# A new hand-written order for a fused cross-attention and PReLU kernel on one Trainium2 core

## The chip, the cores and the metric

The kernel runs on one core of one Trainium2 chip. A core has a matrix engine (TensorE, in the profile PE, with its weight loads as PEld), a vector engine (DVE), a scalar engine (ACT), a general engine (POOL) and a queue engine (SP). Each works through its own list of instructions in order and waits on semaphores of the others. PE reads SBUF and writes PSUM, which has eight banks of 128 x 512 float32; DVE and ACT read PSUM, POOL does not touch it here. The metric is the device time of one execution in microseconds (us), the median of several runs; lower is better.

## The reference

```
scores  = scale * x @ state^T          # per batch b and head h: 512 x 32
xread   = softmax(scores) @ state      # 512 x 64
scores2 = scale * state @ x^T          # 32 x 512
sread   = softmax(scores2) @ x         # 32 x 64
y   = concat([xread, sread], tokens), heads side by side   # (8 * 544) x 512
h   = y @ w_in                         # 512 -> 2048
g   = max(h, 0) + alpha * min(h, 0)
out = g @ w_out                        # 2048 -> 512
```

There are 8 batches, 8 heads, 512 tokens of width 64 and 32 states a head. `x`, `state`, `w_in`, `w_out`, `alpha` and `out` are float32; the kernel works in float16 with float32 sums.

## The kernel before

**Attention.** The 512 tokens of a batch and its states meet once, in a product of scores `sc` (L326), laid out as 128 rows (4 heads x 32 states) by 1024 columns. From it come both softmaxes. Over the states: DVE transposes blocks (`sb`, L357), takes maxima (`smax`), POOL subtracts (`ssh`), ACT takes the exponential (`sexp`), DVE sums (`ssum`), POOL scales (`snorm`, L387), DVE transposes back (`wb`, L397) into the tile `aT`. Over the tokens: DVE takes maxima (`tx`), ACT scales them (`ty`) and takes the exponential with its sum (`te`), DVE inverts the sum (`tsum`), POOL or ACT scales (`tn`), a DMA on SP's queue transposes (`tt`, tile `e2T`), and PE makes the state reads (`rd`, L461, tile `sr_ps`).

**First layer.** `xread @ w_in` is never made as such. PE first makes the products of states and `w_in`, `m` (L486: 8 heads, four column blocks of 512; `m.b.f` is batch b, block f, 8 matmuls), which ACT or DVE casts to SBUF (`mo`, L508). Then each of 16 tiles of h is two matmuls over `aT` (`F.b.jc`, L519). ACT makes the negative part (`N`, L551) and DVE the PReLU (`G`, L569). The state reads of all batches go through the first layer together, as a ninth batch (`F.8`, L528).

**Second layer.** Batch 0 is a plain product (`S`, L588). Batches 1 to 8 use seven products `P` (L668) in place of eight: POOL makes four sums of g for each (`A`, L645, three by itself, one as an accumulating DMA, L621) and sums of `w_out` (`T`); ACT and DVE put the results together (`Q`), and SP stores them (`W`). Pieces of batch 7 are made apart (`M`, L717, and `MO`), so that they can be done late.

**Order.** A string of some 1,180 steps sets everything. A step such as `m.6.1.4.1` names the work and, where it is a PSUM tile, its banks (4 and 1); a last letter names the engine (`a` ACT, `v` DVE, `p` POOL, `d` a DMA). `m` without banks and `sc` use one tile of two banks, tagged `two`. The steps are recorded in the order of the string, and each engine gets its own in that order. So the string also sets what stands behind what on each queue: the loads of x (`lx`) and of the weights (`wi`, `wo`) and the accumulating DMAs are issued from POOL, the transposing DMAs (`xd`, `tt`) and nearly all stores from SP. `Z` steps are matmuls on zeros that only keep PE busy.

`m` and `sc` use PE in tiles of 64 x 32, `rd` and the transposes of the states in tiles of 128 x 64, all the rest in its whole 128 x 128.

Of the kernel before, what the change touches and what calls it, by code (L numbers as in the profile page):

```python
# [17 lines left out]
lx0 id lst stc xc.1.v xc.0.a oma wi.0 lx.1 Z.1.20 stt.0 Z.2.9 xt.0.1.0.1 xt.0.0.0.2 xo.0.1.0.v  # L18
xo.0.0.0.v sto.a Z.0.7 sc.0.0 Z.0.6 xt.0.1.1.3 xt.0.0.1.4 str.0.5 sb.0.0 xo.0.0.1.v xo.0.1.1.a Z.1.4
sc.0.1 smax.0.0 str.1.0 sro.0.a wi.1 sb.0.1 wo.0 smax.0.1 wi.2 ssh.p.0.0 sro.1.a sexp.0.0 Z.1.3 sc.0  # L20
m.0.0.1.2 ssh.p.0.1 mo.0.0.a.0 Z.5.5 m.1.0.3.4 m.2.0.5.0 tm.0 mo.2.0.a.0 ssum.0.0 sexp.0.1
mo.1.0.a.0 mo.2.0.a.1 wo.1 Z.1.12 m.3.0.1.5 Z.3.7 xt.1.1.0.3 snorm.p.0.0 mo.1.0.v.1 te.0.1
mo.3.0.a.1 ssum.0.1 wb.0.0 xt.1.0.0.4 xo.1.1.0.v te.0.0 xo.1.0.0.v wi.3 xt.1.1.1.0 snorm.p.0.1 Z.3.9
f.0.0.0.5 mo.0.0.a.1 xo.1.1.1.v xt.1.0.1.3 wo.2 f.0.2.0.4 tsum.0 m.1.1 wb.0.1 mo.3.0.a.0 xo.1.0.1.v
m.0.1.0.2 mo.1.1.v.0 tn.0.0 mo.0.1.v.0 f.0.2.1 f.0.0.1 mo.1.1.a.1 mo.0.1.a.1 f.0.1.0.1 f.0.1.1
F.0.3.3 m.4.0 N.0.0 N.0.1 F.0.5.2 N.0.2 F.0.4.0 G.0.0 G.0.1 N.0.3 G.0.2 F.0.7.5 N.0.5 N.0.4 G.0.3
S.0.1.0.1 mo.4.0.a.0 S.0.0.0.4 mo.4.0.a.1 G.0.4 S.0.0.1 S.0.1.1 lx.2 N.0.7 m.0.2.3.0 sc.1 G.0.5
mo.0.2.a.0 S.0.2.0.2 wo.3 G.0.7 m.1.2.5.3 mo.0.2.a.1 mo.1.2.a.0 S.0.2.1 sb.1 F.0.6.0 xd.2 mo.1.2.a.1
F.0.8.5 N.0.6 F.0.9.3 tm.1 S.0.1.2 N.0.8 S.0.2.2 S.0.0.2 G.0.6 S.0.1.3 te.1.1 te.1.0 N.0.9 F.0.11.0
# [89 lines left out]
def kernel(  # L119
# [17 lines left out]
    nc = tc.nc  # L137
# [695 lines left out]
```

## Time and profile before

| | |
|---|---|
| median of 3 runs | 210.05 us (210.01 to 210.38) |
| the profiled execution: first to last instruction | 208.5 us |
| median less that span | 1.55 us |
| PE busy | 200.2 us |
| DVE, ACT, POOL busy | 175.2, 145.5, 180.9 us |
| granted PE clock | 1.000 |

The profiled execution has a span and no time of its own beside it. What lies around the span is taken as 1.55 us, by the median. The busy times overlap; a busy PE counts the pipelined end of each matmul too, so the spacing of two groups is what one of them costs.

### The profile page before, as it was taken

Reading aid. Unit: us, or ns where it says so; the run is one execution under the profiler, and the core shown is the slowest. Engines: PE = TensorE matmul, PEld = TensorE weight load, DVE = VectorE, ACT = ScalarE, POOL = GpSimd, SP = SyncE. Lnnn points to the kernel's source line nnn. Section 1 sums busy time; section 2 is a strip of 40 time slices with the busy share of each in tenths; the row PEclk is TensorE's granted clock in tenths of the full one; section 3 lists DMA queues with packets and bytes.
Section 4 is the critical chain, followed back from the end, with each engine's and each line's share of the span. In section 5 each row is a group of like instructions: output and inputs, shape, how many; then the busy total and the mean of one; then the engine's idle time right before and its main releaser. Section 6 shows DMA issues by size and latency. Waiting matters only on the chain.

```text
span 208.5 us, 5136 instructions
## 1 busy us (share of the span) xinstructions
PE 200.2 (96%) x2034; PEld 135.3 (65%) x2034; DVE 175.2 (84%) x273; ACT 145.5 (70%) x291; POOL 180.9 (87%) x119
## 2 busy tenths in 40 slices
PE   7789999999999999999999999999999999999993
PEld 6554344346557775766677776666678777888882
DVE  1697998999999999999999999998995987744431
ACT  4298996699998899988889579778654545451110
POOL 7579948999999999999999999979996972969960
PEclk9999999999999999999999999999999999999999
DMA  6999999599979949999997166035401144234143
GB/s 148 177 204 208 205 203 149 103 132 191 218 144 142 116 58 212 206 126 165 183 225 100 43 146 166 24 82 151 104 0 53 23 78 154 37 63 156 50 153 104
DMA packets 44793, 27.11 MB, mean 130 GB/s; under 512 B 22097, under 2 KB 42465, under 8 KB 44769
## 3 DMA queue, kind: packets, MB, share of 16 engines
q0 software_dynamic: 14192, 12.03, 38.5%
q1 hardware_dynamic: 29872, 14.23, 31.1%
q10 hardware_dynamic: 704, 0.52, 0.8%
q8 instruction: 16, 0.26, 0.5%
q14 instruction: 9, 0.07, 0.1%
HBM read 17.31 MB, written 8.91 MB: 126 GB/s over the span
## 4 chain that ended last, share of the span: by engine, by line
PE 70%; DVE 14%; ACT 5%; DMA 4%; POOL 3%; issue 2%; DVEq 0%; POOLq 0%
PE p L668 41%; PE h L519 18%; DVE gp L569 8%; DMA w_in_sb<-in_moe_w_in_dram 4%; PE h L528 3%; PE m_ps L486 3%; PE sr_ps L461 2%; ACT m L508 1%; DVE aT L397 1%; ACT neg L551 1%; DVE m L508 1%; POOL s L645 1%; ACT e L424 1%; POOL an L387 1%; PE o L588 1%
## 5 line engine op out<-in xcount | busy, mean ns | idle before, releaser
L551 ACT ACTIVATE neg<-h 128x512 f32<-128x512 f32 (+1 forms) x144 | 78.5, 583 | 27.4 <-PE h L519 18.5
L569 DVE SCALAR_TENSOR_TENSOR gp<-neg,oma_sb,h 128x512 f16<-128x512 f32 x128 | 89.0, 735 | 6.7 <-ACT neg L551 6.4
L519 PE MATMUL h<-aT,m 128*128 128x512 f16 x250 | 68.6, 379 | 0.3 <-DVE gp L569 0.3
L645 POOL TENSOR_TENSOR s<-gp,s 128x1024 f16<-128x1024 f16 x28 | 65.7, 2393 | 1.2 <-DVE gp L569 0.6
L668 PEld LDWEIGHTS <-gp 128*128 128x128 f16 x432 | 41.7, 98 | 13.9 <-issue 1.9
L668 PEld LDWEIGHTS <-s 128*128 128x128 f16 x368 | 35.2, 98 | 12.7 <-POOL s L645 1.7
L668 PE MATMUL p<-ws,s 128*128 128x256 f16 x248 | 37.3, 273 | 0.2 <-POOL s L645 0.2
L645 POOL TENSOR_TENSOR s<-gp 128x1024 f16<-128x1024 f16 x14 | 31.6, 2260 | 6.5 <-DVE gp L569 6.4
L519 PEld LDWEIGHTS <-m 128*128 128x128 f16 x250 | 23.6, 98 | 16.1 <-issue 3.3
L668 PE MATMUL p<-ws,gp 128*128 128x256 f16 x224 | 33.6, 273 | 0.0
L508 ACT CAST m<-m_ps 128x512 f16<-128x512 f32 x51 | 28.8, 600 | 4.8 <-PE m_ps L486 3.6
L668 PE MATMUL p<-w_out_sb,gp 128*128 128x256 f16 x208 | 30.6, 273 | 0.0
L371 POOL TENSOR_TENSOR ts<-ts,mx 128x1024 f32<-128x1024 f32 (+1 forms) x9 | 17.1, 1905 | 6.0 <-DVE mx L365 6.0
L668 PE MATMUL p<-w_out_sb,s 128*128 128x256 f16 x120 | 18.3, 273 | 0.0
L387 POOL TENSOR_TENSOR an<-ts,r 128x1024 f16<-128x1024 f32 (+1 forms) x9 | 16.3, 1808 | 1.8 <-DVE r L382 1.8
L588 PE MATMUL o<-w_out_sb,gp 128*128 128x512 f16 x64 | 16.6, 380 | 0.1
L621 POOL DMA_DIRECT2D gp<-gp x14 | 13.2, 962 | 3.4 <-issue 2.9
L569 DVE SCALAR_TENSOR_TENSOR gs<-neg,oma_sb,h 128x256 f16<-128x256 f32 x16 | 7.2, 478 | 8.2 <-ACT neg L551 8.2
L486 PE MATMUL m_ps<-w_in_sb,stT 64*32 64x512 f16 x256 | 11.7, 383 | 0.3 <-DMA w_in_sb<-in_moe_w_in_dram 0.2
L588 PEld LDWEIGHTS <-gp 128*128 128x128 f16 x64 | 5.9, 98 | 8.1 <-issue 1.3
L424 ACT ACTIVATE e<-sc,nb 128x512 f16<-128x512 f32 x16 | 11.0, 693 | 0.1
L699 ACT COPY p<-p 128x512 f32<-128x512 f32 x11 | 6.5, 588 | 6.4 <-PE p L668 6.4
(76 smaller groups left out, 248.9 us busy)
## 6 DMA issues: line engine op xcount, KB each, us to landing
out_dram<-c SPq DMA_DIRECT2D x27, 256.0 KB, 3.1
xg<-in_x_dram POOLq DMA_DIRECT2D x7, 512.0 KB, 8.7
gp<-gp POOLq DMA_DIRECT2D x14, 256.0 KB, 3.6
w_in_sb<-in_moe_w_in_dram POOLq DMA_DIRECT2D x4, 512.0 KB, 11.8
w_out_sb<-in_moe_w_out_dram POOLq DMA_DIRECT2D x4, 512.0 KB, 13.1
out_dram<-osb SPq DMA_DIRECT2D x4, 256.0 KB, 3.0
out_dram<-c SPq DMA_DIRECT2D x3, 128.0 KB, 2.1
x<-in_x_dram SPq DMA_DIRECT2D x1, 256.0 KB, 3.2
```

Source lines behind the costliest of these rows:

```text
L371: engine(e).tensor_tensor(ts, ts, over_blocks(cols(live["mx", b], j, S // N)), ALU.subtract)
L387: engine(e).tensor_tensor(blocks(cols(live["an", b], j, S)), blocks(cols(live["ts", b], j, S)), over_blocks(cols(live["r1", b], j, S // N) ...
L424: nc.scalar.activation(live["e2", b][:, g, :, :], live["sc", b][:, :, :, g, :].rearrange("p r j s -> p (r j) s"), EXP, bias=live["nb", b][ ...
L486: nc.tensor.matmul(t[N * k : N * (k + 1), :], st_head(b, h)[64 * r : 64 * r + 64, :], w_in_sb[64 * r : 64 * r + 64, c, 512 * f : 512 * (f ...
L508: copier(e)(m_tile(b)[:, f, g, :], live["mp", b, f][g])
L519: nc.tensor.matmul(h.rearrange("p (r j s) -> p r j s", r=2, j=2), ms[b][:, f, g, 128 * j : 128 * (j + 1)], weights(b, g), start=(g == 0), ...
L551: nc.scalar.activation(neg, h, RELU, bias=0.0, scale=-1.0)
L569: nc.vector.scalar_tensor_tensor(gt, negs.pop((b, jc)), oma_sb[:, jc : jc + 1], h, ALU.mult, ALU.add)
L588: nc.tensor.matmul(outs[b, q], token_cols(b, jc, q), w_out_sb[:, jc, :], start=(jc == 0), stop=(jc == n_jc - 1),)
L621: nc.gpsimd.dma_start(gp[:, 1, 0], gp[:, 1, 1], accum_op=ALU.add)
L645: engine(e).tensor_tensor(t, x, y, op)
L668: nc.tensor.matmul(chains[chain][:, t, :], lhs, rhs[:, i, :], start=(opens and i == 0 and t == 0), stop=(i == half_k - 1), skip_group_chec ...
```

## The change

The string of steps is replaced. The work is the same, but for two matmuls on zeros fewer (82 to 80). Three scalings of token weights go from POOL to ACT (`tn`), two scalings of token maxima from DVE to ACT (`tm` becomes `tx` and `ty`), and of the copies out of PSUM three results, three state reads and one transpose go from DVE to ACT; the cast of the first states goes to ACT as well. Nine casts of `m` change from DVE to ACT and nine the other way.

```diff
-P.3.3.2 N.4.9 A.4.3.1.p P.4.1.1 G.4.10 P.3.3.3 P.3.4.0 G.4.9 P.4.1.2 G.4.12 P.3.4.1 A.4.1.0.d
-Q.3.c12.v m.6.3 m.6.0.4.5 A.4.2.0.p mo.6.3.a.0 rd.4.3 mo.6.0.v.0 W.Q.3.c12 mo.6.3.a.1 rd.5.0 tsum.6
-wb.5 W.Q.3.c22 tn.6.1.a sc.7 P.3.4.2 mo.6.0.a.1 P.4.1.3 rdo.5.v ssh.p.6 tx.7 P.3.4.3 Q.4.p1.a
...
+Q.3.c12.v W.Q.3.c12 tsum.6 W.Q.3.c21 m.6.1.4.1 mo.6.1.a.0 mo.6.1.v.1 rd.4.2 A.4.3.0.p m.6.3.0.5 mo.6.3.a.1
+mo.6.3.v.0 rd.5.3 rdo.5.a m.6.2.4.1 mo.6.2.a.0 mo.6.2.a.1 sc.7 m.6.0.0.5 mo.6.0.a.0 mo.6.0.a.1 P.4.1.0.3
...
-M.7.2.0.3 M.7.1.0.4 P.8.5.1 W.Q.8.c11 P.8.7.0 P.8.5.2 P.8.7.1 P.8.5.3 P.8.7.2 Q.8.p5.v M.7.1.1
-M.7.2.1 P.8.7.3 M.7.1.2 P.8.3.0 Q.8.c22.v M.7.2.2 M.7.1.3 P.8.3.1 WA.Q.8.c22 MO.7.1.v P.8.4.0
-P.8.3.2 W.MO.7.1 P.8.4.1 P.8.3.3 P.8.4.2 Q.8.c12.v M.7.2.3 P.8.4.3 MO.7.2.v W.Q.8.c12 Q.8.c21.a
-WA.MO.7.2 W.Q.8.c21
+P.8.3.1 P.8.3.2 P.8.3.3 Q.8.c12.v W.Q.8.c12 P.8.4.1 P.8.4.2 P.8.4.3 Q.8.c21.a W.Q.8.c21 M.7.2.0.3 M.7.2.1
+M.7.2.2 M.7.2.3 MO.7.2.v WA.MO.7.2
...
-    def first_states_cast():
+    def first_states_cast(e):
         live["st0"] = consts.tile([128, 2, D], F16, name="st0")
-        nc.vector.tensor_copy(live["st0"], st0_32)
+        copier(e)(live["st0"], st0_32)
```

PE goes from whole tiles into the small tiles of `m`, `sc`, `rd` and the state transposes, and back, 33 times before and 25 times now. With the changes between 64 x 32 and 128 x 64 counted too, its tiling changes 72 times before and 64 times now.

On ACT, around the state products of batch 6 (`m_6` is the cast product, `m_ps6_f_g` block f and half g of it in PSUM, `XS` the state reads, `neg_5_jc` the negative part of tile jc of batch 5), before:

```order
L508 CAST m_6_1840<-m_ps6_3_2079 128x512 x2
L440 ACTIVATE e2_6_2002<-e2_6_2002,r2_6_2003 128x512
L508 CAST m_6_1840<-m_ps6_0_1_2089 128x512
L699 COPY p1_4_2209<-p1_4_2034 128x512
L472 CAST XS_86<-sr_ps4_2101 128x4x32
L551 ACTIVATE neg_5_0_2228<-h_5_0_2217 128x512
```

and now:

```order
L499 CAST m_6_2087<-m_ps6_1_0_2077 128x512
L499 CAST m_6_2087<-m_ps6_3_1_2126 128x512
L463 CAST XS_86<-sr_ps5_2137 128x4x32
L499 CAST m_6_2087<-m_ps6_2_0_2171 128x512
L499 CAST m_6_2087<-m_ps6_2_1_2172 128x512
L499 CAST m_6_2087<-m_ps6_0_0_2200 128x512
L499 CAST m_6_2087<-m_ps6_0_1_2201 128x512
L463 CAST XS_86<-sr_ps4_2090 128x4x32
L542 ACTIVATE neg_5_5_2252<-h_5_5_2225 128x512
```

All four blocks of batch 6 are now cast in one run, with both state reads among them, ahead of the first negative part of batch 5; before, blocks 2 and 1 stood elsewhere.

On SP's queue, from the first result of batch 1 on (`xT_4` is the transposed x of batch 4, `e2T_2` the transposed token weights of batch 2), before:

```order
L579 DMA out_0_dram<-c11_1_1068 256x1x256
L304 DMA_TRANSPOSE xT_4_1071<-xg_4_901 128x16x128
L446 DMA_TRANSPOSE e2T_2_1145<-e2_2_778 128x8x128
L446 DMA_TRANSPOSE e2T_3_1324<-e2_3_1161 128x8x128
L579 DMA out_0_dram<-c22_1_1217 256x1x256
```

and now:

```order
L570 DMA out_0_dram<-c11_1_1094 256x1x256
L437 DMA_TRANSPOSE e2T_2_1249<-e2_2_763 128x8x128
L295 DMA_TRANSPOSE xT_4_1297<-xg_4_901 128x16x128
L295 DMA_TRANSPOSE xT_5_1317<-xg_5_987 128x16x128
L437 DMA_TRANSPOSE e2T_3_1333<-e2_3_1203 128x8x128
```

`xT_4` has moved behind `e2T_2`, which waits for ACT's scaling of the token weights of batch 2; `xT_5` has moved up to it.

More of the change, by code (lines that the diff above doesn't have):

```diff
@@ new lines @@
+mo.4.0.a.1 S.0.1.0.2 S.0.1.1 m.0.2.3.1 mo.0.2.a.0 mo.0.2.a.1 S.0.0.1 sc.1 tx.1 T.0.1.p m.1.2.3.5 sb.1
+mo.1.2.a.0 mo.1.2.a.1 F.0.7.0 N.0.7 G.0.7 smax.1 ssh.p.1 ty.1 F.0.8.1 F.0.11.3 N.0.11 G.0.11 te.1.0 te.1.1
+T.1.0.p tsum.1 N.0.8 G.0.8 S.0.1.2 S.0.2.0.5 S.0.2.1 S.0.2.2 F.0.9.0 N.0.9 G.0.9 S.0.0.2 m.0.3 mo.0.3.a.1
+mo.0.3.a.0 S.0.1.3 S.0.0.3 F.0.10.3 m.1.3 mo.1.3.v.1 N.0.10 G.0.10 sexp.1 ssum.1 S.0.2.3 snorm.p.1 F.0.13.0
+tn.1.0.a F.0.14.1 S.0.1.4 S.0.2.4 N.0.14 G.0.14 mo.1.3.a.0 F.0.12.3 N.0.12 G.0.12 N.0.13 G.0.13 S.0.2.5
@@ new lines @@
+T.1.1.p S.0.0.4 S.0.0.5 tn.1.1.a F.0.15.1 N.0.15 m.2.1 mo.2.1.a.1 mo.2.1.a.0 S.0.3.0.3 S.0.2.6 S.0.0.6 G.0.15
+S.0.2.7 O.0.2.a W.O.0.2 tt.1 T.3.0.p T.2.0.p m.3.3.1.0 mo.3.3.a.0 mo.3.3.a.1 sc.2 S.0.0.7 O.0.0.a W.O.0.0 wb.1
+F.1.2.5 tx.2 ty.2 sb.2 lx.3 N.1.2 G.1.2 F.1.1.1 N.1.1 F.1.3.0 te.2.1 N.1.3 S.0.1.5 S.0.1.6 S.0.1.7 O.0.1.a
+smax.2 G.1.1 ssh.p.2 F.1.9.4 G.1.3 te.2.0 N.1.9 G.1.9 S.0.3.1 S.0.3.2 F.1.8.5 F.1.0.2 N.1.0 G.1.0 F.1.10.1
+N.1.10 S.0.3.3 G.1.10 N.1.8 G.1.8 sexp.2 ssum.2 rd.0.0 rdo.0.a m.2.3 rd.1.4 F.1.6.2 rdo.1.a F.1.7.1 N.1.7
@@ new lines @@
+P.1.6.0 F.2.15.0 G.2.10 P.1.6.1 N.2.15 G.2.15 F.2.13.4 N.2.13 G.2.13 mo.3.2.a.0 P.1.2.2 F.2.0.3 P.1.2.3
+Q.1.c11.v xd.3 W.O.0.1 sc.3 m.4.1.0.2 sb.3 tx.3 tn.2.1.a N.2.0 G.2.0 mo.4.1.a.0 mo.4.1.a.1 A.1.2.1.p P.1.6.2
+P.1.6.3 Q.1.u.a tn.2.0.a A.1.1.0.d F.2.9.5 A.1.1.1.d P.1.5.0.0 A.1.4.0.p P.1.5.1 F.2.12.2 P.1.5.2 F.2.2.4
+W.Q.1.c11 P.1.5.3 smax.3 ty.3 N.2.9 P.1.7.0 P.1.7.1 G.2.9 N.2.2 N.2.12 G.2.12 G.2.2 Q.1.p5.a te.3.0 T.2.1.p
+P.1.7.2 te.3.1 tsum.3 P.1.7.3 Q.1.c22.v F.2.11.5 F.2.5.2 N.2.11 G.2.11 N.2.5 G.2.5 A.1.4.1.p P.1.3.0 P.1.3.1
@@ new lines @@
+P.1.3.2 ssh.p.3 sexp.3 ssum.3 tt.2 rd.2.4 rdo.2.a m.4.3.5.3 mo.4.3.a.0 mo.4.3.a.1 xd.4 sc.4 tn.3.0.a xd.5
+P.1.4.0 P.2.2.0.4 P.1.4.1 tn.3.1.a tt.3 F.2.6.3 N.2.6 sb.4 tx.4 F.2.14.5 N.2.14 G.2.14 A.2.3.0.p ty.4 G.2.6
+te.4.1 te.4.0 P.1.3.3 T.3.1.p P.1.4.2 P.1.4.3 Q.1.c21.a P.2.1.0.2 P.2.2.1 P.2.2.2 snorm.p.3 wb.3 m.3.1.3.5
+m.5.1 P.2.1.1 mo.3.1.a.1 mo.3.1.a.0 P.2.2.3 smax.4 Q.1.c12.v F.3.1.5 N.3.1 G.3.1 F.3.10.3 N.3.10 G.3.10
+F.3.8.1 N.3.8 G.3.8 P.2.1.2 P.2.1.3 Q.2.p1.a Q.2.c11.v F.3.11.5 N.3.11 G.3.11 W.Q.1.c21 W.Q.1.c12 W.Q.1.c22
@@ new lines @@
+mo.4.2.a.0 mo.4.2.a.1 snorm.p.4 wb.4 F.3.15.0 F.4.2.5 N.4.2 G.3.14 sb.5 tx.5 A.2.4.0.p P.2.3.0 N.3.15 G.3.15
+P.2.4.3 A.3.3.1.p Q.2.c21.a F.4.7.1 N.4.7 G.4.7 ty.5 te.5.1 te.5.0 G.4.2 P.2.3.1 P.2.3.2 F.4.12.2 P.2.3.3
+Q.2.c12.v F.4.1.0 N.4.1 G.4.1 tsum.5 F.4.14.1 N.4.14 G.4.14 F.4.4.5 N.4.4 G.4.4 F.4.0.3 N.4.0 G.4.0 tn.5.1.a
+F.4.3.4 N.4.3 G.4.3 P.3.1.0.0 P.3.1.1 N.4.12 G.4.12 F.4.11.1 N.4.11 G.4.11 P.3.1.2 P.3.2.0.5 P.3.1.3 Q.3.p1.a
+smax.5 P.3.2.1 F.4.13.4 N.4.13 P.3.2.2 m.5.3.2.3 mo.5.3.a.0 m.5.0 mo.5.0.a.0 tsum.4 mo.5.3.v.1 P.3.2.3
@@ new lines @@
+Q.3.c11.v W.Q.3.c11 W.Q.2.c21 F.4.6.1 N.4.6 G.4.6 G.4.13 mo.5.0.a.1 F.4.5.2 N.4.5 G.4.5 F.4.10.3 N.4.10 G.4.10
+W.Q.2.c12 A.3.3.0.p A.3.2.0.p tn.5.0.a tt.5 P.3.6.0 P.3.6.1 lx.7 A.3.2.1.p P.3.6.2 P.3.6.3 Q.3.u.a sc.6 xd.7
+m.7.3.4.1 mo.7.3.v.1 tx.6 sb.6 tn.4.0.a m.5.2.2.5 mo.5.2.a.1 tn.4.1.a tt.4 mo.5.2.a.0 P.3.7.0 P.3.7.1 F.4.9.1
+N.4.9 P.3.7.2 G.4.9 A.3.1.0.d P.3.5.0.5 A.3.1.1.d A.3.4.0.p smax.6 ssh.p.5 sexp.5 P.3.5.1 P.3.7.3 P.3.5.2
+P.3.5.3 Q.3.p5.a Q.3.c22.v F.4.15.1 N.4.15 ty.6 F.4.8.2 N.4.8 A.4.3.1.p P.3.3.0 P.3.3.1 mo.7.3.a.0 G.4.15
@@ new lines @@
+Q.4.c11.v W.Q.4.c11 A.4.1.0.d ssh.p.6 sexp.6 ssum.6 N.5.15 te.7.0 F.5.7.2 F.5.3.0 N.5.3 P.4.6.0 G.5.15 P.4.6.1
+F.5.6.4 N.5.6 G.5.6 A.4.2.1.p P.4.6.2 F.5.1.1 tn.6.1.p snorm.p.6 N.5.7 G.5.7 te.7.1 tsum.7 P.4.6.3 P.4.5.0.5
+P.4.5.1 P.4.5.2 P.4.5.3 Q.4.u.a P.4.7.0 P.4.7.1 G.5.3 N.5.1 G.5.1 tn.6.0.a wb.6 F.5.8.1 N.5.8 G.5.8 F.5.4.0
+Q.4.p5.a P.4.7.2 P.4.7.3 Q.4.c22.v N.5.4 G.5.4 smax.7 F.5.9.2 N.5.9 G.5.9 tn.7.0.a F.5.13.1 N.5.13 G.5.13
+F.5.10.4 N.5.10 G.5.10 P.4.4.0 P.4.4.1 A.4.4.0.p P.4.3.0 P.4.3.1 P.4.4.2 A.4.4.1.p tn.7.1.a F.6.2.2 tt.7 N.6.2
```

139 lines of the change are left out of this document (49 added, 90 removed).

## The prediction, made before the changed kernel was run

> **What bounds the kernel now.** I read the busy times first, then what PE waited for after its start, and then PE's own timeline beside the chain of waits.
>
> ```profile
> span 208.5 us, 5136 instructions
> PE 200.2 (96%) x2034; PEld 135.3 (65%) x2034; DVE 175.2 (84%) x273; ACT 145.5 (70%) x291; POOL 180.9 (87%) x119
> PE p L668 <- POOL s L645: 0.2, 1, 0.2
> ```
>
> The last row is the whole answer for PE's waits between 25 and 205 us: one wait of 0.2 us. From 25 us on PE sets the time, although DVE and POOL are nearly full too. The same matmuls are made after the change, so it can win only what PE spends beside them: the start, changes of tiling, and the end after the last matmul. Each new wait of PE costs its full length.
>
> ```profile
> 66.22 0.60 PE L668 MATMUL p<-ws,s 128*128 128x256 f16 x4
> 66.75 0.41 PE L486 MATMUL m_ps<-w_in_sb,stT 64*32 64x512 f16 x8
> 67.09 0.61 PE L668 MATMUL p<-ws,s 128*128 128x256 f16 x4
> ...
> 75.92 0.68 PE L461 MATMUL sr_ps<-e2T,xg 128*64 128x32 f16 x32
> 76.53 0.63 PE L486 MATMUL m_ps<-w_in_sb,stT 64*32 64x512 f16 x16
> 77.09 0.61 PE L668 MATMUL p<-w_out_sb,gp 128*128 128x256 f16 x4
> ...
> 89.56 0.41 PE L326 MATMUL sc<-xT,stT 64*32 64x256 f16 x16
> 89.78 0.40 PE L486 MATMUL m_ps<-w_in_sb,stT 64*32 64x512 f16 x8
> 71.63 3.06 PE p L668 x28
> 80.75 2.16 PE h L519 x10
> ```
>
> The last two rows, from the chain of waits, give 3.06/28 = 0.109 us for a P matmul and 2.16/10 = 0.216 for one of h. Four P from 66.22 end their issue at 66.66; `m` starts 0.09 later. Its 8 matmuls take 0.34 to the next group. Sixteen take 0.56 (76.53 to 77.09), so 8 more cost 0.22 and leaving costs 0.34 - 0.22 = 0.12. One visit to small tiles costs 0.21, one change of tiling about 0.105. From `sc` into `m`, which have the same tiling, nothing is lost (89.56 to 89.78 is 0.22).
>
> **The change part by part.** *Joined stretches.* After the first tile of h of batch 1, the old string changes PE's tiling 43 times and the new one 32 times: 11 x 0.105 = **-1.15 us**. The visits fall more, but `m` and `rd` now alternate inside them, and each alternation is paid as well. Bounds: 0, if a joined stretch waits inside for a bank as long as it saves, and -1.6. I take the full count, because every change in the rows costs about the same.
>
> *The start.* These rows of the old start carry the replay:
>
> ```profile
> 9.62 2.22 ACT L294 COPY stT<-st_ps 128x896 f16<-128x896 f16 x2 [0.70 <-PE st_ps L260]
> 14.92 0.71 ACT L424 ACTIVATE e<-sc,nb 128x512 f16<-128x512 f32 x1
> 17.94 1.29 DVE L508 CAST m<-m_ps 128x512 f16<-128x512 f32 x2
> 18.66 1.07 ACT L508 CAST m<-m_ps 128x512 f16<-128x512 f32 x2 [0.83 <-DVE m L508]
> 19.62 3.07 ACT L551 ACTIVATE neg<-h 128x512 f32<-128x512 f32 x6
> 20.27 4.70 DVE L569 SCALAR_TENSOR_TENSOR gp<-neg,oma_sb,h 128x512 f16<-128x512 f32 x7 [1.05 <-ACT neg L551]
> 28.09 1.13 DVE mx L365
> 36.05 1.25 DVE aT L397
> 38.36 0.61 PE L519 MATMUL h<-aT,m 128*128 128x512 f16 x2
> L317 DVE COPY xT<-xT_ps 128x512 f16<-128x512 f16 x7 | 2.6, 406 | 0.5 <-PE xT_ps L312 0.5
> L442 POOL TENSOR_SCALAR e<-e,r 128x512 f16<-128x512 f16 x6 | 9.7, 1665 | 0.1
> ```
>
> The first exponential now precedes the two state copies, so these end near 12.7 instead of 11.84. Behind them ACT has an exponential (0.6), five casts (1.07/2 each), the scaling that comes from DVE (0.2) and two token exponentials (0.7 each): 4.9 us, so the first negative part starts near 17.6, and the first PReLU, behind DVE's own casts and copies, near 18.4, not 20.27. That lead of 1.9 is spent again. Up to the end of `smax` of batch 1 DVE has 8 PReLUs (4.70/7 each), one cast (1.29/2), two copies of transposed x that stood ahead of the first PReLU before (0.4 each, L317), an inverted sum (0.2), and block transpose, token maxima and state maxima (1.2 each, as the state maxima of 28.09): 5.4 + 0.65 + 0.8 + 3.6 + 0.2 = 10.6, so it ends near 29.0; before at 28.09 + 1.13 = 29.2. Then two more PReLUs stand ahead of `wb.1`: near 36.9 instead of 36.05. The first h of batch 1 comes near 38.8 instead of 38.36, with equal work of PE behind it: **+0.45**, uncertain by 0.8 either way, since several waits of 0.1 to 0.4 lie in between.
>
> *The scalings and copies* that leave POOL (3 x 1.67, L442) and DVE go to ACT, whose load grows by about 6.6 us (thirteen operations of 0.2 to 0.7) and stays near 152 of 208. None of them stands on PE's path; they give POOL and DVE room and cost nothing while ACT's idle time (63 us) covers them; if it does not, it is the second rival.
>
> *The transposing DMAs.*
>
> ```profile
> 19.19 0.94 POOL L175 DMA_DIRECT2D xg<-in_x_dram  x1
> 32.29 3.17 SPq L304 DMA_TRANSPOSE xT<-xg  x1
> 39.90 0.41 PE L326 MATMUL sc<-xT,stT 64*32 64x256 f16 x16
> 60.48 4.09 SPq L304 DMA_TRANSPOSE xT<-xg  x1
> 69.81 0.41 PE L326 MATMUL sc<-xT,stT 64*32 64x256 f16 x16
> 64.68 12.14 SPq L446 DMA_TRANSPOSE e2T<-e  x2
> DMA to landing us min/median/max: 4.7/6.1/6.9
> DMA to landing us min/median/max: 3.1/3.9/7.6
> ```
>
> (The landing rows are those of `xT` and of `e2T`.) The load of x of batch 2, issued at 19.19, had landed by 32.29, behind the weights on the same queue. It is issued some 2 us earlier now, but the same bytes go first, so its transpose lands no later than 32.3 + 6.1 = 38.4 and `sc.2` stands near 37.7 on PE: 0 to 0.6, I take **+0.3**. `xT_4` had 69.81 - 60.48 = 9.3 us to its use (`sc.4` is at 69.81). Now it stands behind `e2T_2`, which waits for ACT's second scaling of batch 2. That comes behind a negative part, two casts and the copy of `u` of batch 1; `u` needs the last `P.1.6`, which ends near 62.3 on PE in the new order (38.8 and 23.5 us of matmuls and tiling changes at the rates above). The copy is done near 63.6, the scaling near 64.4. With 1.3 us in the queue for `e2T_2`, `xT_4` is issued near 65.7. PE has 5 tiles of h (5 x 0.43), 11 groups of P (11 x 0.44) and a visit of `rd` and `m` (0.95) from 62.3 to `sc.4`: 70.2. At 4.7, 6.1 and 6.9 us to landing PE waits 0.2, 1.6 and 2.4. No load is in flight at that time in the new order, so I take **+0.2**.
>
> The Trainium skill, "DMA: Bandwidth & Descriptors", section "Queues, rings and completion order", says that each DMA engine consumes the descriptors of a ring in ring order, which would put `xT_4` wholly behind `e2T_2`. The trace is in line with it where one transpose follows another: the `e2T` issued at 64.68, right behind an `xT`, is the one of 7.6 us; but a load of x was in flight too.
>
> *The end.*
>
> ```profile
> 204.40 0.28 PE L717 MATMUL o<-w_out_sb,gp 128*128 128x128 f16 x2
> 204.51 0.38 PE L668 MATMUL p<-ws,gs 128*128 128x256 f16 x2
> 204.72 0.28 DVE L728 TENSOR_TENSOR osb<-p,o 128x128 f32<-128x128 f32 x1
> 204.93 0.37 ACT L703 COPY c<-p 128x256 f32<-128x256 f32 x1 [4.24 <-PE p L668]
> 205.03 0.38 ACTq L582 DMA_DIRECT2D out_dram<-osb  x1
> out_dram<-osb ACTq DMA_DIRECT2D x1, 64.0 KB, 2.2
> ```
>
> The last P matmuls end their issue at 204.73, the span ends 3.8 later, behind ACT's copy and a store by SP. In the new order the 8 small matmuls of the last piece come last; two of them take 0.11 here (204.40 to 204.51), so the path of the copy starts 0.44 before PE ends. The piece's own path, from 204.62 by DVE and ACT's queue, lands at 205.03 + 2.2 = 207.2, 2.6 after its matmul, and is shorter. The end shrinks by **-0.45**.
>
> Sum: -1.15 + 0.45 + 0.3 + 0.2 - 0.45 = -0.65. Against the profiled 208.5 this is a span of 207.85, and with 1.55 around it **209.4 us**.
>
> **The rivals.** *Transposes come late.* `sc.4` waits 1.6 to 2.4 rather than 0.2, and `sc.2` 0.6 rather than 0.3. For it: PE is without slack, and `xT_4` has lost half of its lead. Against it: the landing of 4.7 exists, and waits elsewhere would move `sc.4` back and hide it. 209.4 + 0.3 + 1.4 to 2.2 = 211.1 to 211.9, priced at 211.4; it makes the kernel slower by more than my bound from a landing of 5.5 us on. By the Trainium skill's ring order, with 3.1 for `e2T_2` and 4.7 behind it, `xT_4` would land at 72.2 and `sc.4` wait 2.0, which is this case.
>
> *Copies of joined stretches stall PE.* In the stretch of batch 6 ACT has six casts and two copies of reads in a row, 6 x 0.53 + 2 x 0.44 = 4.1 us, and no negative part meanwhile. PE has about 6.6 us (the stretch 2.7, four groups of P, five tiles of h) until it needs the first bank that the delayed negative part and PReLU free. With a result's copy (0.6) ahead, and negative part, PReLU and hand-overs behind (0.5 + 0.7 + 0.5), 6.4 are used. So it decides from 0.2 us of backlog on ACT. For it: ACT carries more than before; against it: it idles for a quarter of the time even so. At 0.6 us there and 0.2 in each of five other stretches 209.4 + 1.6 = 211.0, slower.
>
> *The start gains.* If the lead of 1.9 us at the first PReLU isn't wholly spent, as PE fills its early gaps better, by 1.2: 208.2. For it: the old start has waits of PE up to 21 us; against it: DVE has more to do in it now.
>
> *The change doesn't do what it says.* If a joined stretch saves nothing, since each `m` in it waits for the bank of the one before, 209.4 + 1.15 = 210.55: the same, or slower by a hair.
>
> **How the numbers follow.** Forecast 0.46 (209.4; own range 208.7 to 210.0); start gains 0.11; late transposes 0.21; stalls at copies 0.14; nothing saved 0.08. A difference of less than 0.2% (0.42 us, so 209.63 to 210.47) is about what a measurement of this kernel can't tell from none. Faster: 0.40 of the forecast and the start's 0.11, 0.51. Same: 0.05 of the forecast, 0.02 each of the two slower rivals, 0.05 of nothing saved, 0.14. Slower: 0.35. The range of 8 in 10 reaches from 207.9, inside the start's case, to 211.6, inside the late transposes.
>
> **What would show it.** Right: PE's tiling changes at 0.1 each as before; groups of `m` that follow `rd` without a wait; `sc.4` with less than 0.5 us of wait; the first h of batch 1 near 38.8; 3.3 us from PE's last matmul to the end. Wrong: waits of PE after 25 us that add up to over 1 us, above all ahead of `sc`, or h behind DVE's PReLU after a joined stretch. A landing of `xT_4` 6 us or more after its issue would make the first rival true; a first h of batch 1 before 38 the third.

## The result, and the profile after

The changed kernel takes 211.61 us (median of 7 runs, 210.30 to 212.54) beside 210.01 for the kernel before: slower by 0.83%, ratio 1.0083 [1.0057, 1.0108]. Its profiled execution took 211.98 us with a span of 209.9. Executions over 1.5% above the fastest of their kernel (two of `load_behind`, one each of `load_and_tail` and `scalings_back` below) count in no ratio.

First the page after, and PE's waits from 25 us on (line waited for, total, times, longest). Line numbers are 9 less than before.

```profile
span 209.9 us, 5132 instructions
PE 200.6 (96%) x2032; PEld 138.0 (66%) x2032; DVE 171.6 (82%) x262; ACT 150.0 (71%) x305; POOL 176.0 (84%) x116
PE p L659 <- DMA gp<-gp: 1.6, 1, 1.6
PE sc L317 <- DMA xT<-xg: 0.4, 1, 0.4
```

PE waits 2.0 us there, against 0.2 before, and 1.6 of them in one place that the prediction does not name: ahead of the products that read a token sum made by an accumulating DMA (`A.1.1.0.d`, batch 1). The timeline around it, from POOL and PE, with the landing of that first DMA sum from the tile's view (three equal numbers: one transfer):

```profile
55.02 0.94 POOL L166 DMA_DIRECT2D xg<-in_x_dram  x1
55.98 2.14 POOL L636 TENSOR_TENSOR s<-gp,s 128x1024 f16<-128x1024 f16 x1
58.05 1.88 POOL L612 DMA_DIRECT2D gp<-gp  x2
62.62 0.59 PE L510 MATMUL h<-aT,m 128*128 128x512 f16 x2
64.78 1.05 PE L659 MATMUL p<-ws,gp 128*128 128x256 f16 x8 [1.57 <-DMA gp<-gp]
DMA to landing us min/median/max: 6.7/6.7/6.7
```

The new order puts the load of x of batch 5 (`lx.5`, 512 KB, at 55.02) 3.0 us ahead of the two sums on POOL's queue. PE needs the first one 5.2 us after its issue, and it lands after 6.7. Before, that load stood behind both sums (63.21), and the first sum, issued at 55.69, landed 3.4 us later. In the timeline of the kernel before, with the landing of that sum and then that of all 14 such sums:

```profile
55.69 0.95 POOL L621 DMA_DIRECT2D gp<-gp  x1
63.21 1.55 POOL L175 DMA_DIRECT2D xg<-in_x_dram  x1
DMA to landing us min/median/max: 3.4/3.4/3.4
DMA to landing us min/median/max: 3.2/3.6/5.4
```

The end after, and the end of its chain of waits:

```profile
204.87 0.61 PE L708 MATMUL o<-w_out_sb,gp 128*128 128x128 f16 x8
205.96 0.37 ACT L694 COPY c<-p 128x256 f32<-128x256 f32 x1 [8.50 <-DMA out_dram<-c]
206.32 0.29 DVE L719 TENSOR_TENSOR osb<-p,o 128x128 f32<-128x128 f32 x1 [1.49 <-DMA out_dram<-c]
206.65 0.38 ACTq L573 DMA_DIRECT2D out_dram<-osb  x1
...
201.79 0.70 DVE c L697
202.49 0.02 issue
202.51 3.69 DMA out_dram<-c
```

The last copy and the last addition do not follow their matmuls: each waits for a store to land. All results share five buffers (`osb`), and in the new order the results of batches 7 and 8 come so close together that the last two have to wait until stores hand buffers back. PE's last matmul ends its issue at 204.87 + 8 x 0.055 = 205.31, and 4.6 us follow, where the prediction had 3.3 and the kernel before 3.8.

Where the span's 1.4 us come from, then, by the two traces:

| | predicted | measured |
|---|---|---|
| up to the first h of batch 1, with the wait of `sc.2` (38.36 to 39.28) | +0.75 | +0.92 |
| changes of tiling behind it (11 x 0.11) | -1.15 | -1.2 |
| wait for the DMA sum | none | +1.57 |
| POOL's wait of before | none | -0.2 |
| wait of `sc.4` | +0.2 | 0 |
| from PE's last issue to the end | -0.45 | +0.82 |
| short gaps between PE's matmuls (what is left over) | none | -0.5 |

The first h of batch 1 is the row `39.28 1.46 PE L510` of the timeline. From there to PE's last issue lie 166.03 us, 166.37 before; less the waits of 1.57 and 0.2 that is 164.46 against 166.17, so 1.7 less. The matmuls in between, priced by the rows, come to the same in both. A visit to small tiles for 16 `m` takes 0.65 in both traces, of which the `m` are 0.43, so a change still costs 0.11, and 11 of them make 1.2. The other 0.5 are gaps of the old order that the view of waits does not list. That view counts idle time from the end of the last matmul, and a P matmul is shown for 0.27 us although the next one starts after 0.109; so it leaves out the first 0.16 us of each gap. In the timeline of the kernel before, for example, two P take 0.44 where 0.22 would do, and two h and the change to `sc` take 0.67 where 0.52 would do:

```profile
202.87 0.38 PE L668 MATMUL p<-w_out_sb,s 128*128 128x256 f16 x2
203.31 0.38 PE L668 MATMUL p<-ws,gs 128*128 128x256 f16 x2
...
39.23 0.59 PE L519 MATMUL h<-aT,m 128*128 128x512 f16 x2
39.90 0.41 PE L326 MATMUL sc<-xT,stT 64*32 64x256 f16 x16
```

Time less span is 2.1 us in this execution, where the prediction took 1.55. Executions of the kernel before that have both numbers give about 1.8 (209.52 with a span of 207.7), so 0.3 us of the loss lie outside the span, and 0.2 of the miss were a poor estimate.

### The profile page after: what moved, and what is told of

It is laid out like the page before. It is cut to its first block, busy times and chain, and to the rows that moved or that the text cites. A ratio compares the mean times of both kernels' runs of the same rounds, so it can differ in the third digit from the quotient of the medians.

```text
span 209.9 us, 5132 instructions
## 1 busy us (share of the span) xinstructions
PE 200.6 (96%) x2032; PEld 138.0 (66%) x2032; DVE 171.6 (82%) x262; ACT 150.0 (71%) x305; POOL 176.0 (84%) x116
## 4 chain that ended last, share of the span: by engine, by line
PE 78%; DMA 10%; POOL 5%; DVE 4%; issue 1%; ACT 0%; ACTq 0%; DVEq 0%
PE p L659 39%; PE h L510 21%; PE o L579 4%; POOL s L636 4%; PE h L519 3%; PE m_ps L477 3%; DMA gp<-gp 3%; DMA xT<-xg 3%; PE sr_ps L452 2%; DMA out_dram<-c 2%; DMA x<-in_x_dram 2%; PE z L236 1%; PE sc L317 1%; PE xT_ps L303 1%; POOL xg L166 1%
## 5 line engine op out<-in xcount | busy, mean ns | idle before, releaser
L542 ACT ACTIVATE neg<-h 128x512 f32<-128x512 f32 (+1 forms) x144 | 76.9, 586 | 23.8 <-PE h L510 17.9
L510 PE MATMUL h<-aT,m 128*128 128x512 f16 x250 | 65.9, 379 | 0.0
L636 POOL TENSOR_TENSOR s<-gp,s 128x1024 f16<-128x1024 f16 x28 | 64.3, 2308 | 1.6 <-PE p L659 1.2
L510 PEld LDWEIGHTS <-m 128*128 128x128 f16 x250 | 24.0, 98 | 17.5 <-issue 1.2
L659 PE MATMUL p<-ws,s 128*128 128x256 f16 x248 | 33.4, 273 | 0.0
L636 POOL TENSOR_TENSOR s<-gp 128x1024 f16<-128x1024 f16 x14 | 30.7, 2193 | 3.1 <-DVE gp L560 1.8
L659 PE MATMUL p<-ws,gp 128*128 128x256 f16 x224 | 29.7, 273 | 1.6 <-DMA gp<-gp 1.6
L659 PE MATMUL p<-w_out_sb,gp 128*128 128x256 f16 x208 | 27.5, 273 | 0.0
L659 PE MATMUL p<-w_out_sb,s 128*128 128x256 f16 x120 | 16.4, 273 | 0.0
L697 DVE TENSOR_TENSOR c<-p,p 128x512 f32<-128x512 f32 x13 | 8.9, 682 | 2.8 <-PE p L659 2.3
L694 ACT COPY c<-p 128x512 f32<-128x512 f32 (+1 forms) x6 | 3.3, 552 | 10.8 <-DMA out_dram<-c 8.5
```

The lines of the kernel that those rows point to most:

```text
L510: nc.tensor.matmul(h.rearrange("p (r j s) -> p r j s", r=2, j=2), ms[b][:, f, g, 128 * j : 128 * (j + 1)], weights(b, g), start=(g == 0), ...
L542: nc.scalar.activation(neg, h, RELU, bias=0.0, scale=-1.0)
L636: engine(e).tensor_tensor(t, x, y, op)
L659: nc.tensor.matmul(chains[chain][:, t, :], lhs, rhs[:, i, :], start=(opens and i == 0 and t == 0), stop=(i == half_k - 1), skip_group_chec ...
```

## The experiments

A ratio is to the kernel before on the same chip. Its median there was 209.9 to 210.0.

**The load behind the two sums.** Changed kernel; here and below steps stand as in the string.

```diff
-m.2.2.3.0 mo.2.2.a.1 mo.2.2.a.0 lx.5 m.3.2 F.1.13.5
+m.2.2.3.0 mo.2.2.a.1 mo.2.2.a.0 m.3.2 F.1.13.5
...
-A.1.1.0.d F.2.9.5 A.1.1.1.d P.1.5.0.0
+A.1.1.0.d F.2.9.5 A.1.1.1.d lx.5 P.1.5.0.0
```

> The changed kernel with one step moved: the load of x of batch 5 goes behind the two token sums of batch 1 that DMA adds on the same queue, instead of ahead of them. Theory (the load in flight makes the first sum land 6.7 us after its issue, and PE waits 1.6 us for it): the sum lands 3.3 to 4.5 us after its issue, PE's wait for it is gone, the time falls by 1.2 to 1.6 to about 210.2, and the runs spread less. Rival (the two sums are issued too late, or too close to one another, and the load has no part in it): the sum still lands 6 us or more after its issue, PE waits at least 0.6 us, time above 210.9. Second rival (the wait only covers another, of the state scores of batch 4 for their transposed x): PE's wait moves to the scores and the time falls by less than 0.5.

Measured: 211.12 us, ratio 1.0066 [1.0039, 1.0093]. The first sum lands in 3.4 us and PE's wait for it is gone, so the first rival falls. But two other waits have come up, in PE's timeline:

```profile
69.07 0.68 PE L452 MATMUL sr_ps<-e2T,xg 128*64 128x32 f16 x32 [0.54 <-DMA e2T<-e]
70.77 0.41 PE L317 MATMUL sc<-xT,stT 64*32 64x256 f16 x16 [0.68 <-DMA xT<-xg]
```

The load, issued at 57.83 and landed 9.5 us later, now runs beside the transposes of batches 2 and 4, which take 5.9 and 6.1 us to landing (4.5 for the latter with the load ahead). Of the 1.57 us some 0.5 are kept by the medians, which is less than the intervals tell apart, and 0.3 between the first h of batch 1 and PE's last issue in the traces (165.7 for 166.0). The second rival is right in the main: the wait moves, to the scores and to the state reads.

**The load 8 us earlier.** Changed kernel.

```diff
-G.1.7 lx.4 F.1.11.5
+G.1.7 lx.4 lx.5 F.1.11.5
...
-m.2.2.3.0 mo.2.2.a.1 mo.2.2.a.0 lx.5 m.3.2 F.1.13.5
+m.2.2.3.0 mo.2.2.a.1 mo.2.2.a.0 m.3.2 F.1.13.5
```

> The changed kernel with the load of x of batch 5 moved the other way: directly behind the load of x of batch 4, some 8 us earlier, so that it has landed before the two DMA sums of batch 1 are issued and does not run beside the transposes of batches 2 and 4 either. Theory: the first sum lands in 3.3 to 4.5 us, PE does not wait for it, and neither the state reads nor the scores that waited 0.5 and 0.7 us with the load behind wait now: 1.2 to 1.7 us less than the changed kernel, near 210.1 (0 to 0.2% above before). Rival (the gain of the changed place is lost wherever the load goes, since its 512 KB delay something else on PE's path): waits of 0.8 us or more appear elsewhere after 40 us, time above 210.8.

Measured: 209.44 us, ratio 0.998 [0.9955, 1.0006], 2.2 us less than the changed kernel and 0.7 better than expected; it can't be told from the kernel before. POOL's timeline and the sum's landing:

```profile
45.51 1.83 POOL L166 DMA_DIRECT2D xg<-in_x_dram  x2
...
57.68 1.85 POOL L612 DMA_DIRECT2D gp<-gp  x2
DMA to landing us min/median/max: 3.4/3.4/3.4
```

With this load moved up by some 8 us, the view of PE's waits is empty from 25 us to the end. From the first h of batch 1 to PE's last issue the trace has 164.3 us for 166.0, 1.7 less; another 0.5 of the 2.1 by which the spans differ lies ahead of that stretch, where the two orders are the same. One misplaced load was worth about the whole loss.

**The same load, early in the kernel before.**

```diff
-P.1.2.1 A.1.3.1.p G.1.15
+P.1.2.1 lx.5 A.1.3.1.p G.1.15
...
-F.2.1.3 lx.5 P.1.5.2
+F.2.1.3 P.1.5.2
```

> The kernel before with the load of x of batch 5 moved ahead of the last sum on POOL that stands before the first of the two DMA sums of batch 1, which puts it 3 us ahead of that DMA sum on the queue as in the changed kernel. Theory: the DMA sum lands 6 us or more after its issue and PE, which has some 4.4 us of lead there, waits 1.5 to 2.3 us in front of the product that reads it; slower by 0.7 to 1.1%. Rival (the load has no part in it): the sum lands in 3.4 to 4.5 us, PE waits under 0.3 us, time within 0.2% of before.

Measured: 210.68 us, ratio 1.0042 [1.0027, 1.0057]. The load lies 3.0 us ahead again, and the sum lands in

```profile
DMA to landing us min/median/max: 5.4/5.4/5.4
```

which is 2.0 slower than without it, but less than the 6 expected; PE reads that sum 5.5 us after its issue, where the expectation had 4.4, so it is just in time. PE's wait is in front of another sum, one of POOL's own, since the issue of the load (0.94 us) stands ahead of it now:

```profile
58.89 0.61 PE L658 MATMUL p<-ws,s 128*128 128x256 f16 x4 [0.79 <-POOL s L635]
```

A landing of 5.4 alone would prove little: one of the 14 sums of the kernel before took as long (issued at 117.87, the last load at 90.21). But the time of landing follows the load. In the four runs whose load stands 3.0 us ahead, the first sum lands 1.2 to 1.4 us after the load does (64.7 after 63.4 in the changed kernel, 61.1 after 59.9 here, 65.8 after 64.4 in `start_before`, 64.8 after 63.6 in `tail_buffers`), whether that is 5.4 or 6.8 us after its issue. So the load does delay the sum in this order too; how much of that reaches PE depends on the lead that the order leaves.

**The buffers at the end.** Changed kernel, order untouched.

```diff
-        osb = moe.tile(shape, F32, name=f"{name}_{b}", tag="osb", bufs=5)
+        tag, bufs = ("neg", 4) if b == B else ("osb", 5)
+        osb = moe.tile(shape, F32, name=f"{name}_{b}", tag=tag, bufs=bufs)
...
-        osb = moe.tile([128, hi - lo], F32, name=f"osb_{b}_{i}", tag="osb", bufs=5)
+        osb = moe.tile([128, hi - lo], F32, name=f"osb_{b}_{i}", tag="neg", bufs=4)
```

> The changed kernel, its order untouched; the last results (those of batch 8 and the pieces M.7) are written to the four buffers of the negative parts, idle by then, instead of the five shared result buffers. Theory (the last result and the last piece wait up to 1.5 us for stores to give buffers back): ACT's copy and DVE's addition at the end follow their matmuls, 3.3 to 3.9 us lie between PE's last matmul and the end instead of 4.6, time lower by 0.7 to 1.3. Rival (the stores themselves are the bound at the end, buffers or not): 4.3 us or more remain and the time falls by less than 0.3.

Measured: 210.76 us, ratio 1.0044 [1.0022, 1.0067]. From PE's last issue (206.0) to the end (209.7) 3.7 us remain, as expected. The stretch ahead of it, from the first h of batch 1 on, is 0.7 us longer in this execution than in the changed kernel's (166.8); the DMA sums' waits in it are 2.1 us.

**Load behind and buffers together.** Both edits of `load_behind` and `tail_buffers`.

> Both edits together. Theory: the two stalls lie one behind the other on PE's path, so the gains add: 1.9 to 2.9 us less than the changed kernel, about 209.2, faster than the kernel before by 0.4 or more. Rival (they hide one another, or PE's freed time runs into a wait for the transposed x of batch 4): less than 1.3 us gained, no faster than before.

Measured: 211.52 us, ratio 1.0068 [1.0044, 1.0091]: missed by 2.3 us. The expectation had taken the sum's 1.57 as gained, of which `load_behind` keeps little. That the buffers' 0.9 does not show here either stays open: the profiled execution ran at a granted clock of 0.986, so its rows can't be compared.

**The earlier load and the buffers together.**

> The run with the load directly behind that of batch 4, and the last results in the buffers of the negative parts. Theory: PE does not change, the last copy and the last piece no longer wait up to 1.7 us for stores, 3.6 to 3.9 us from PE's last matmul to the end instead of 4.7: about 208.6, faster than the kernel before by 0.5 to 0.9%. Rival (the stores on SP's queue are the bound there): 4.4 us or more at the end, within 0.3 us of the run without the buffers.

Measured: 208.57 us, ratio 0.9934 [0.992, 0.9947], with runs from 208.49 to 208.92: faster than both kernels. Its page, and the end of its timeline:

```profile
span 206.9 us, 5130 instructions
...
202.90 0.61 PE L709 MATMUL o<-w_out_sb,gp 128*128 128x128 f16 x8
203.14 0.37 ACT L695 COPY c<-p 128x256 f32<-128x256 f32 x1 [7.65 <-PE p L659]
203.55 0.29 DVE L720 TENSOR_TENSOR osb<-p,o 128x128 f32<-128x128 f32 x1 [0.68 <-PE o L709]
```

Copy and addition wait for PE now; from 203.34 to 206.9 are 3.6 us, against 4.7 with the earlier load alone.

**Last piece last, in the kernel before.**

```diff
-M.7.2.0.3 M.7.1.0.4 P.8.5.1
+M.7.1.0.4 P.8.5.1
...
-Q.8.c12.v M.7.2.3 P.8.4.3 MO.7.2.v W.Q.8.c12 Q.8.c21.a WA.MO.7.2 W.Q.8.c21
+Q.8.c12.v P.8.4.3 W.Q.8.c12 Q.8.c21.a W.Q.8.c21 M.7.2.0.3 M.7.2.1 M.7.2.2 M.7.2.3 MO.7.2.v WA.MO.7.2
```

(`M.7.2.1` and `M.7.2.2` leave their places too.)

> The kernel before with one edit: the four steps of the last piece of batch 7, its addition and its store stand behind the last result of batch 8. What the prediction took for the end: PE's last matmul to the end shrinks from 3.8 to 3.3 us, 0.45 less time, since the longer path of the last copy starts earlier. Rival (the last piece and the last copy wait for stores to give back result buffers, as in the changed kernel): 4.2 us or more at the end and 0.4 to 0.9 us more time.

Measured: 210.03 us, ratio 1.0002 [0.9989, 1.0016]. From 204.88, PE's last issue, to 208.4 are 3.5 us, and no buffer is waited for. Half of the term that the prediction put down is there on the trace (0.25 of 0.45), and none of it in the time that can be told. The stretch ahead of it is 0.3 us longer (166.6 for 166.3), and PE's view has a new wait, for DVE's sums of results:

```profile
PE p L658 <- DVE c L696: 0.3, 1, 0.3
```

**Joined stretches cut again.** On the run with the earlier load; one of eight places:

```diff
-m.3.1.3.5 m.5.1 P.2.1.1
+m.3.1.3.5 P.2.1.1 m.5.1
```

> The run with the load directly behind that of batch 4, with eight of the joined stretches of small tiles cut in two again: one step of h or of the products of the token part, which stood behind the stretch, moves in between two of its steps. PE's tiling then changes 76 times instead of 64, with the same matmuls. Theory of the prediction: 12 changes at 0.105 us make 1.3 us more. What the two traces make of it (PE gains some 1.7 us over 11 changes): 12 at 0.15 make 1.8 us more. Rival (a joined stretch saves nothing, as it waits inside for banks and casts): less than 0.4 us more, or less time.

Measured: 212.25 us, ratio 1.0109 [1.0092, 1.0126], 2.8 us above the run it was cut from. From the first h of batch 1 to PE's last issue it takes 167.2 us (38.34 to 205.54), the uncut run 164.3 (38.81 to 203.11): 2.9 more. Both prices in the expectation were too low, but not because a change costs more. In the view of waits three of the moved steps now wait themselves, 1.0 us in all, the two longest for results that come from ACT; and the spacing of the starts shows more, as with `h` at 109.57, which four P (0.44) precede by 0.67:

```profile
107.07 0.41 PE L317 MATMUL sc<-xT,stT 64*32 64x256 f16 x16
107.82 0.60 PE L659 MATMUL p<-ws,s 128*128 128x256 f16 x4 [0.33 <-ACT u L690]
...
108.90 0.61 PE L659 MATMUL p<-ws,s 128*128 128x256 f16 x4
109.57 0.59 PE L510 MATMUL h<-aT,m 128*128 128x512 f16 x2
...
118.36 0.68 PE L452 MATMUL sr_ps<-e2T,xg 128*64 128x32 f16 x32
119.58 0.60 PE L659 MATMUL p<-w_out_sb,gp 128*128 128x256 f16 x4 [0.54 <-ACT XS L463]
```

By that spacing PE stands in six places for 0.60, 0.40, 0.24, 0.22, 0.13 and 0.07 us, all at or right behind a cut, and that is 1.6 us more than in the uncut run. The other 1.3 are 0.11 for each of the 12 changes. The rival, that joining saves nothing, falls. A single change shows the same price in the rows. In the fastest version, inside one joined stretch:

```profile
115.56 0.41 PE L477 MATMUL m_ps<-w_in_sb,stT 64*32 64x512 f16 x8
115.90 0.68 PE L452 MATMUL sr_ps<-e2T,xg 128*64 128x32 f16 x32
...
117.46 0.41 PE L477 MATMUL m_ps<-w_in_sb,stT 64*32 64x512 f16 x8
117.69 0.40 PE L317 MATMUL sc<-xT,stT 64*32 64x256 f16 x16
117.91 0.40 PE L477 MATMUL m_ps<-w_in_sb,stT 64*32 64x512 f16 x8
118.24 1.05 PE L659 MATMUL p<-w_out_sb,gp 128*128 128x256 f16 x8
```

Eight `m` take 0.22 to 0.23 when the tiling stays (117.46 to 117.69), 0.34 and 0.33 when it changes behind them: 0.11 a change, as before.

**The old start with the new rest.** The first 200 steps of the old order, then what is left in the new one; and the same with the earlier load. With few steps in common around the seam no diff of a few lines shows it.

> A program in two parts: the order of the kernel before up to its first tiles of h of batch 1 (200 steps, 38 us), then all that is left in the changed order, with two pairs of banks exchanged so that the parts fit. Theory (the changed start costs PE 0.9 us up to there, and is the part that spreads the runs, because it asks for the transposed x of batch 1 earlier): 0.5 to 1.2 us faster than the changed kernel, with runs within 1 us of one another; PE's wait for the DMA sum of batch 1 stays (1 to 2 us), and so do 4.4 us or more at the end. Rival (the start costs nothing, the spread comes from later): no faster than the changed kernel, spread of 2 us as there.

> The start of the kernel before, the rest in the changed order, and the load of x of batch 5 directly behind that of batch 4. Theory: the two gains add, no wait for the DMA sum: 209.0 to 209.6, faster than before by 0.2 to 0.5%. Rival (the wait for the sum only hides another of about its length): within 0.4 us of the run with the old start alone.

Measured: 212.81 us, ratio 1.0135 [1.0112, 1.0159], and 211.38, ratio 1.007 [1.0047, 1.0093]. Both miss: the old start makes it slower by 1.2 and 1.9 us than the new start does. In the first, PE waits 1.39 and 1.28 us for the two sums, which landed 6.2 and 8.3 us after their issue. In the second those are gone, and the seam itself shows two waits for ACT's copies:

```profile
40.27 0.41 PE L476 MATMUL m_ps<-w_in_sb,stT 64*32 64x512 f16 x8 [0.67 <-ACT osb L751]
45.23 1.18 PE L509 MATMUL h<-aT,m 128*128 128x512 f16 x4 [0.60 <-ACT osb L751]
```

By the spacing of the starts these two and four shorter gaps up to 52 us make some 2.1 us, as much as the 1.9; so these runs do not tell what the old start is worth. The profiled executions tell more: the first h of batch 1 comes at 38.1 to 39.3 us in the seven that have the new start, 38.75 on average, and at 37.4 to 38.4 in the three that have the old one, 38.0 on average. The +0.92 of the table is from one pair of them. Time less span is 1.7 to 1.9 us in both runs, as in the kernel before, and 1.8 to 2.3 in the runs with the new start. But it is 1.7 to 1.9 in `scalings_back` below as well, so the order of the start alone does not make it; what does was not tried.

**The scalings on their old engines.** On the fastest version: four scalings of token weights back from ACT to POOL, one the other way, the scaled maxima of batches 0 and 1 on DVE again. Four of the nine edits to the string:

```diff
-tn.1.0.a
+tn.1.0.p
...
-F.4.10.3 N.4.10 G.4.10 W.Q.2.c12 A.3.3.0.p A.3.2.0.p tn.5.0.a tt.5
+F.4.10.3 N.4.10 G.4.10 W.Q.2.c12 A.3.3.0.p A.3.2.0.p tn.5.0.p tt.5
...
-tn.6.1.p
+tn.6.1.a
...
-tn.7.0.a
+tn.7.0.p
```

> The best version so far (load of batch 5 directly behind that of batch 4, last results in the buffers of the negative parts) with the scalings on their engines of before: the four scalings of token weights that went to ACT back on POOL (1.67 us each there), the one that went to POOL back on ACT, and the scaled token maxima of batches 0 and 1 on DVE in one step again. Theory of the prediction (they lie beside PE's work wherever they run): within 0.3 us, no wait of PE over 0.3 us after 40 us. Rival (POOL is so full that the move is what makes room): PE waits 1 us or more for sums of POOL or for results of DVE, 1 to 3 us slower.

Measured: 211.12 us, ratio 1.0061 [1.0029, 1.0093], 2.5 us above the fastest version. So the scalings cost nothing on ACT, as predicted, but where they run does matter. One of POOL's scalings now stands ahead of the load of x of batch 7:

```profile
98.47 1.56 POOL L432 TENSOR_SCALAR e<-e,r 128x512 f16<-128x512 f16 x1
99.99 0.97 POOL L165 DMA_DIRECT2D xg<-in_x_dram  x1
...
113.87 1.26 SPq L436 DMA_TRANSPOSE e2T<-e  x1
...
117.05 0.68 PE L451 MATMUL sr_ps<-e2T,xg 128*64 128x32 f16 x32 [0.99 <-DMA e2T<-e]
```

In the fastest version the load is issued at 98.36 and the transposed weights at 112.30, 1.6 us earlier each; they land 3.2 later, 0.4 ahead of the joined stretch that reads them at 115.90. Here that stretch waits 0.99. The way from the one to the other is not shown whole: the transpose before it starts to be issued at nearly the same time in both (106.89 here, 106.59 there), but its issue takes 3.54 us here and 1.72 there. POOL's DMA sums, 1.7 us later here, were landing then, which may be why. In the profiled executions PE loses 1.95 us against the fastest version between the first h of batch 1 and its last issue; beside the 0.99 the spacing of the starts shows 0.34 ahead of an `h` at 48.04 and 0.41 ahead of one at 131.59. The executions spread from 210.08 to 212.94, so the sign is surer than the size.

**The transpose of batch 4 in front again.** On the fastest version.

```diff
-W.Q.1.c11 P.1.5.3
+W.Q.1.c11 xd.4 P.1.5.3
...
-mo.4.3.a.1 xd.4 sc.4
+mo.4.3.a.1 sc.4
```

> The best version so far with the transposing DMA of x of batch 4 ahead of that of the token weights of batch 2 on SP's queue, right behind the first result store, as it stands in the kernel before. Theory (where it stands in the changed order it lands 4.5 us after its issue and 0.3 us before its use, so nothing is to be gained): within 0.3 us. Rival, the first of the prediction (the changed place costs time on PE in most executions): 0.6 us or more faster. Second rival (in front it delays the token weights of batch 2, and the state reads wait): 0.4 us or more slower.

Measured: 208.78 us, ratio 0.9951 [0.9929, 0.9974], 0.2 us from the fastest version: nothing to be gained there.

## Why the prediction was wrong, step by step

It said faster at 0.51, 209.4 us, and a range up to 211.6; the kernel is slower and lies a hair beyond the range. Its sum put the span 0.65 us lower; it came out 1.4 higher.

**The step that failed** is in the part on the transposing DMAs. "No load is in flight at that time in the new order" was said of 65.7 us, and was true there only because the load of batch 5 had moved up by 8 us. The sentence used that as relief for `xT_4` and did not ask what the load had moved past: two accumulating DMAs on its own queue, of which PE reads the first 5.2 us after its issue. Such sums landed 3.2 to 5.4 us after their issue before, so the slowest of them would already have been late. The sum has no term for this wait; it costs 1.57 us in the profiled execution, and with the load moved out of the way the kernel is 2.2 us faster.

**The end** is the second step that failed, with the wrong sign: -0.45 forecast, +0.82 measured. The working followed the matmuls and the paths of two results, and left out who holds the buffers that these results are written to. In the changed order the end is 3.6 to 3.8 us with buffers free, 0.3 to 0.5 more than the prediction had, and 4.1 to 4.7 with the five shared ones.

**Joined stretches** held: 1.15 predicted, 11 x 0.11 = 1.2 by the rows, and the run with stretches cut again gives the same price once its waits are taken out. What the prediction did not see is 0.5 of short gaps in the old order, since it took the view of waits for the whole of what PE waited.

**Start, `sc.2`, `sc.4`** held: +0.92 for +0.75 in this pair of executions, and +0.7 by the averages; `xT_4` issued at 65.61 for a forecast 65.7. It lands 4.5 us after its issue, and in the fastest version `sc.4` runs at 70.28 without a wait (70.2 forecast). So the first rival names the right kind of event, a transfer that is late, in the wrong place. Beside it stood a rule of the Trainium skill ("DMA: Bandwidth & Descriptors", section "Queues, rings and completion order": each engine takes a ring's descriptors in ring order, though a later one may finish its write before an earlier one). That `xT_4` would stand wholly behind `e2T_2` and land at 72.2 was the prediction's own step from there: `e2T_2` landed at 67.8 and `xT_4` at 70.1, which neither shows nor excludes the rule. What the runs do show is slower landing beside a 512 KB load on POOL's queue, with the sum behind it as well as, in `load_behind`, with transposes on another queue. That the sum lands 1.2 to 1.4 us after the load each time looks like a queue served in order; the slower transposes do not come from that, and no run has the load on another queue to tell the two apart.

**Copies on ACT**, the second rival, did not happen: no wait behind the stretch of batch 6. **The scalings** were costed at nothing for lack of a wait on PE; undone, the kernel is 2.5 us slower, of which the trace shows 0.99 in one wait.

## What to carry to other kernels

When an order is changed, follow each load to the transfers that it now precedes within about 8 us, on its queue and beside it, and hold their landing with a load in flight (5.4 to 8.3 us here for sums of 256 KB, one of which takes 3.4 without) against the lead that the reader has; a sum behind a load landed 1.2 to 1.4 us after it here. At the end of a program, ask of each result which buffer it is written to and which store has to land first. And cost a moved operation by the deadline of what stands behind it on both queues, not by whether its engine has room: a scaling of 1.56 us on POOL moved the load and the DMA sums behind it by 1.6 to 1.7. When a sum of waits does not meet the time, take the spacing of the starts, since the view of waits leaves out short gaps.

## What was not expected of the hardware

One and the same DMA, which adds 256 KB within SBUF, landed 3.4 us after its issue with no load within 7 us ahead of it, and 5.4 to 6.8 us after it (8.3 for the second of a pair) with a 512 KB load issued 3.0 us ahead on the queue; that load took 7.2 to 8.6 us itself, and 9.5 beside two transposes. In the kernel before, too, a load of x (issued at 48.72, landed 9.0 us later) was still in flight when the sum was issued at 55.69, and the sum landed 1.4 us behind it; it still took no more than 3.4 us, since it was issued only 2.0 us before the load landed. The executions of the changed kernel differ by 2.2 us among themselves, those of the kernel before by 0.7 beside it and by 0.8 to 1.9 on the other chips; `load_earlier` spreads by 3.0 and `load_earlier_tail` by 0.4 in five executions. What makes them differ was not followed.
